# Nyström attention feeding a mixture of experts: the C path's scores for both head halves in one group, the expert chosen on all partitions, and a plan with measured group times

## Chip, cores and metric

One core of a Trainium2 chip runs the whole kernel. The metric is the device time of one execution in microseconds, and for several runs their median. "Rows" below are lines of the profile of one execution. TensorE is PE (its weight loads are PEld), VectorE is DVE, ScalarE is ACT, GpSimd is POOL, SyncE is SP.

## What is computed

The reference takes q, k and v of 4 batches, 8 heads, 576 tokens and 64 columns, and forms landmarks as means over 18 tokens, 32 for each head:

```python
A = sm(q, k_lm)
Bm = sm(q_lm, k_lm)
C = sm(q_lm, k)
Z = Bm.transpose(0, 1, 3, 2) / (norm1 * norminf + 1e-06)
for _ in range(6):
    Z = 2 * Z - Z @ Bm @ Z
x = A @ Z @ C @ v          # (4 * 576, 512)
```

`sm` is a softmax over the last axis of the scaled product, with the row maximum taken off first. The 2304 rows then go through a mixture of 8 experts with a capacity of 576 each: the gate `x @ w_gate` picks one expert a token, tokens past an expert's capacity are dropped, and the output is the token's probability times `relu(x @ w1[e]) @ w2[e]`.

## The kernel before

**Tiling.** Eight heads lie in two halves `x` (or `g`) of 64 partitions, times four places `j` in the free dimension; the product of a 64-row half with 32 landmarks uses a 64x32 tile of TensorE. For each batch `b` six generators issue the work: `loads`, `landmarks`, `chain` (the inverse, six steps `pp`), two `cpath` (C and its product with v), two `apath` (A, by token halves), `route` (gate, expert choice, capacity). For each of the first three batches a feed-forward pass runs with the one expert that most of the batch chooses: `w1load`, `gstage`, `ffn` with its two layers (`hps`, `yps`), `wload`, `wsplit`. The expert is guessed on the chip: `guess` for batch 0 from sums over v, `count` (inside `route`) for batches 1 and 2, both ending in `pick`, which leaves the number `ei` (with it the weights are fetched) and a row `fst` of eight flags on one partition. Batch 3 has no pass of its own here; its output rows are zeroed, and a branch behind the plan would run whatever is left over.

**The C path before.** `cpath(b, g)` runs once for each head half. Eight products of 288 columns (L494) fill a two-bank tile `psC`; VectorE takes the maximum over all 576 tokens (L499) and scales it (L501); ScalarE takes the exponential with its sum (L504); four transposes and a fifth for the last 64 tokens (L524) bring it to tokens on partitions, copied out by L529 and L533; twenty products with v (L541) fill `cvp`, and L546 drains it, times the inverse sum from L509 and L510. The landmark product `mtp` (L605) needs both halves' result and the finished inverse (L480). The A path (L563) takes both halves in one group, for one half of the tokens at a time.

**Expert row.** `fsp` (L699) is a product with ones that copies `fst` to all partitions just before the factors of the output rows (L702) are formed.

**Order.** The order of work is planned before the kernel runs: `weave` (L83) simulates five queues (P for TensorE, V, A, G, and D for transfers) with a cost for every step, hops between engines (`HOP`) and priorities from `CFG`, and emits each instruction when its step is chosen, so each engine's instruction order is what the plan gave it. The strings in `CFG` choose an engine for steps that have a choice (`lm` for the landmark sums, `aw`, `al`, `ce`, `rx`, `lo`, `ye`). `sw` is a penalty on a TensorE step whose kind (FFN or other) differs from the one before. Where the plan sees TensorE idle, `fill` (L923) puts dummy products `wps` (L929) into the gap, one for each 216 ns of it, until the first product of the second FFN layer is issued.

Of the kernel before, what the change touches and what calls it, by code (L numbers as in the profile page):

```python
# [18 lines left out]
class Step:  # L19
    def __init__(self, eng, cost, deps=(), order=(), name=None, res=None, nres=1, keep=False, free=None, prev=True, start=0, prio=None, fast=False,  # L20
                 port=False, issue=430):
        self.issue = issue
# [6 lines left out]
    sw=4000,  # L29
    sc='VAAA',  # L30
    rx='VGVGVVVGGVGVVVVVGGGVVGGGGGGVVGVVGVVGVVVVVGGVGVGV',
    look=0.05,
    tg='fftftfttttfttftfttfttttt',
    ce='AAAVAVAV',
    pa='ffsssfff',
    aw='GVGVGGVGVVGGVVGV',
    ye='VVAAAVVAAAVAAVAV',
    lm='VVVVVGGGGVGVGVVV',
    al='GVGVVG',
    lo='VGVVVGVVGVGVVVGGVVVVVGVV',  # L40
    pr=[
# [4 lines left out]
    ],  # L46
    fr=[
        [-1093, 102, -1718, 504, 1080, 901],
        [-5297, 910, -3998, 1924, 1728, -3915],
        [-5242, -5815, -509, 4290, -4277, 441],  # L50
    ],
    sp=[-640, -5473, -5831],
    ah=[-5437, -2470, -2263],
    rl=[-485, -2407, -4653],
    ev=[596, -2196, 1681],
)
HOP = dict(P=205, V=85, A=105, G=0, D=2000)
# [25 lines left out]
def weave(streams, banks, fill=None):  # L83
# [7 lines left out]
    fast = False  # L91
# [21 lines left out]
    while ready:  # L113
# [21 lines left out]
        t, s = min((c for c in cand[eng] if c[0] <= lim), key=lambda c: (c[1][5] + swap * (c[1][2].fast != fast), c[0]))  # L135
# [4 lines left out]
        if eng == "P":  # L140
            if step.fast != fast:
                t += 60
            fast = step.fast
# [7 lines left out]
        t = end + HOP[eng] if step.cost else end  # L151
# [20 lines left out]
def nystrom_moe(ctx: ExitStack, tc: tile.TileContext, q, k, v, vtail, wgate, w1, w2, out, cap):  # L172
# [59 lines left out]
    wg = const.tile([128, NP, NG, 32], F32, name="wg")  # L232
# [45 lines left out]
    def loads(b):  # L278
# [3 lines left out]
        for g in range(2):  # L282
            for nm, src in (("q", q), ("k", k)):
                busy = ([f"psA{b - 2}0", f"psA{b - 2}1", f"psC{b - 2}0"] if nm == "q" else
                        [f"psC{b - 2}0", f"psC{b - 2}1", f"psA{b - 2}0"])
                for j0, j1 in ((2 * g, 2 * g + 1), (2 * g + 1, 2 * g + 2)) if one else ((2 * g, 2 * g + 2),):
                    yield Step("D", 820 * (j1 - j0), deps=[*busy, f"bp{b - 2}"] if b > 1 else (), prev=False,
# [74 lines left out]
    def guess(b):  # L362
# [3 lines left out]
        for x in range(NG):  # L366
            for ch in range(2):
                if x or ch:
                    yield Step("P", 300, prev=False, deps=[f"ld{b}{x}v"], name=f"gs{b}" if x and ch else None)
# [629 lines left out]
```

## Time and profile before

| | |
|---|---|
| Median of 3 runs | 205.97 us (205.31 to 206.12) |
| The profiled execution | 205.63 us, span 203.9 us |
| TensorE matmul busy | 196.2 us, 96% (of it the dummies of L929: 23.2) |
| VectorE busy | 127.9 us, 63% |
| ScalarE busy | 78.0 us, 38% |
| GpSimd busy | 66.0 us, 32% |
| DMA | 31.95 MB, 157 GB/s mean |

Busy time of TensorE includes the dummies and is modelled at the ends of pipelined matmuls, so it tells less than the other engines' figures; the mean duration of one matmul is longer than the step from one to the next. The chain of waits joins the pieces of work that ended last, so the length of a piece there is the time that it takes out of the span.

### The profile page before, as it was taken

To read this page: it belongs to the slowest core of one execution; us is meant where nothing else is said; L and a number is where in the kernel's file an instruction comes from. 1 tells how busy PE (TensorE), PEld (TensorE's weight loads), DVE (VectorE), ACT (ScalarE), POOL (GpSimd) and SP (SyncE) were. 2 spreads that over 40 slices of the span, in tenths; PEclk is the share of its full clock that TensorE was granted. 3 is DMA by queue.
4 is the path that set the end of the run, shared out by engine and by line. 5 is a ranking of instruction groups with operands and counts; after the bars stand their busy time and mean duration, and the time that the engine had idled before them with its cause. 6 is when DMAs were issued, how large, how long until landed. Compare 5 with 4: busy or idle time off the path is not lost.

```text
span 203.9 us, 5705 instructions
## 1 busy us (share of the span) xinstructions
PE 196.2 (96%) x2301; PEld 140.1 (69%) x2302; DVE 127.9 (63%) x381; ACT 78.0 (38%) x178; POOL 66.0 (32%) x110
## 2 busy tenths in 40 slices
PE   7999999999999999999999999999999999999980
PEld 2435454757787766776887776777887789788870
DVE  3789964899798686947888678794024685200100
ACT  2014142944762213326486555410155757111000
POOL 7017599850610238326167453000000506000000
PEclk9999999999999999999999999999999999999998
DMA  6999799934500159897563095301117000020021
GB/s 204 387 412 359 273 293 393 320 95 148 158 3 0 26 167 318 291 359 239 169 206 120 0 301 217 108 17 63 51 51 257 5 3 2 3 67 31 35 82 37
DMA packets 17924, 31.95 MB, mean 157 GB/s; under 512 B 1568, under 2 KB 9632, under 8 KB 17888
## 3 DMA queue, kind: packets, MB, share of 16 engines
q1 hardware_dynamic: 17744, 31.46, 44.9%
q8 instruction: 20, 0.33, 0.7%
q14 instruction: 16, 0.13, 0.2%
q10 hardware_dynamic: 144, 0.03, 0.1%
HBM read 26.77 MB, written 4.72 MB: 154 GB/s over the span
## 4 chain that ended last, share of the span: by engine, by line
PE 94%; DVE 3%; ACT 0%; issue 0%
PE yps L874 33%; PE hps L816 21%; PE wps L929 10%; PE yps L879 5%; PE psC L494 4%; PE pp L471 3%; PE gps L596 3%; PE cvp L541 3%; PE ctp L524 3%; PE psA L563 3%; PE ltp L641 1%; PE bbp L454 1%; PE mtp L605 1%; DVE lmq L329 1%; PE bp L402 1%; PE pp L468 1%
## 5 line engine op out<-in xcount | busy, mean ns | idle before, releaser
L874 PE MATMUL yps<-wh,hx 128*128 128x512 f32 (+1 forms) x208 | 62.8, 378 | 0.0
L874 PEld LDWEIGHTS yps<-wh,hx 128*128 128x128 f32 x208 | 38.1, 189 | 8.1 <-issue 0.5
L874 PE MATMUL yps<-wl,hx 128*128 128x512 f32 (+1 forms) x104 | 38.8, 373 | 0.0
L816 PE MATMUL hps<-ah,gh 128*128 128x288 f32 x96 | 30.5, 318 | 0.0
L839 POOL TENSOR_TENSOR hx<-rr,hx 128x288 fp32r<-128x288 f32 (+2 forms) x31 | 19.4, 645 | 28.3 <-ACT hx L830 23.2
L816 PE MATMUL hps<-al,gh 128*128 128x288 f32 x96 | 28.3, 295 | 0.0
L816 PE MATMUL hps<-ah,gl 128*128 128x288 f32 x96 | 28.3, 295 | 0.0
L929 PE MATMUL wps<-wt 128*128 128x512 bf16 x87 | 23.2, 404 | 1.3 <-DVE half L222 1.3
L874 PEld LDWEIGHTS yps<-wl,hx 128*128 128x128 f32 x104 | 19.6, 188 | 3.3
L889 ACT ACTIVATE yo<-yps,fac 128x512 f32<-128x512 f32 (+1 forms) x9 | 6.0, 666 | 40.5 <-PE yps L874 37.9
L816 PEld LDWEIGHTS hps<-ah,gh 128*128 128x128 f32 x96 | 18.0, 188 | 3.6 <-ACT hx L830 1.0
L755 POOL TENSOR_TENSOR wl<-w2t,wh 128x512 fp32r<-128x512 f32 x7 | 9.1, 1295 | 33.8 <-ACT wh L749 33.7
L755 DVE TENSOR_TENSOR wl<-w2t,wh 128x512 fp32r<-128x512 f32 x17 | 12.6, 749 | 9.7 <-issue 9.3
L816 PEld LDWEIGHTS hps<-al,gh 128*128 128x128 f32 x96 | 18.1, 188 | 0.0
L816 PEld LDWEIGHTS hps<-ah,gl 128*128 128x128 f32 x96 | 18.0, 188 | 0.0
L929 PEld LDWEIGHTS <-wt 128*128 128x128 bf16 x87 | 8.1, 103 | 11.6 <-issue 4.2
L891 DVE TENSOR_SCALAR yo<-yps,fac 128x512 f32<-128x512 f32 (+1 forms) x4 | 2.7, 684 | 20.1 <-PE yps L874 20.1
L841 DVE SCALAR_TENSOR_TENSOR hx<-hps,hx 128x224 fp32r<-128x224 f32 (+2 forms) x41 | 13.1, 348 | 2.9 <-ACT hx L833 2.6
L749 ACT CAST wh<-w2t 128x512 fp32r<-128x512 f32 x24 | 14.4, 617 | 0.9 <-DMA w2t<-in_w 0.7
L833 ACT ACTIVATE hx<-hps 128x288 fp32r<-128x288 f32 x27 | 11.1, 410 | 9.1 <-PE hps L816 8.8
L504 ACT ACTIVATE Cx<-psC,cs 128x576 f32<-128x576 f32 x8 | 5.9, 743 | 19.6 <-DVE cs L501 19.6
L775 ACT CAST gh<-gps 128x512 fp32r<-128x512 f32 x12 | 7.0, 587 | 13.3 <-PE gps L596 13.2
(173 smaller groups left out, 323.1 us busy)
## 6 DMA issues: line engine op xcount, KB each, us to landing
w1t<-in_w SPq DMA_DIRECT2D x12, 512.0 KB, 5.5
w2t<-in_w SPq DMA_DIRECT2D x24, 256.0 KB, 5.8
vm<-in_v SPq DMA_DIRECT2D x8, 512.0 KB, 7.0
qt<-in_q SPq DMA_DIRECT2D x6, 576.0 KB, 6.8
kt<-in_k SPq DMA_DIRECT2D x6, 576.0 KB, 7.6
out<-yo SPq DMA_DIRECT2D x11, 256.0 KB, 2.0
qt<-in_q SPq DMA_DIRECT2D x4, 288.0 KB, 4.6
kt<-in_k SPq DMA_DIRECT2D x4, 288.0 KB, 5.7
```

The lines of the kernel that those rows point to most:

```text
L471: nc.tensor.matmul(pp[y, x], lhsT=PQ[y, x, 0], rhs=PQ[y, x, 0:3:2], start=True, stop=True)
L494: nc.tensor.matmul(t[32 * j:32 * j + 32, a, :HS], lhsT=lmt[b]["q"][y, j], rhs=st[b]["k"][y, j, HS * a:HS * a + HS], start=True, stop=True)
L749: nc.scalar.copy(wh, w2t)
L755: (nc.gpsimd if e == "G" else nc.vector).tensor_tensor(wl, w2t, wh.bitcast(F32), ALU.subtract)
L775: nc.scalar.copy(gh, pg[:, :, 0:FH])
L816: nc.tensor.matmul(ps[:, :HS], lhsT=wt[:, g, fs], rhs=a[:, g, ss], start=(n == 0), stop=(n == 3 * NG - 1))
L833: nc.scalar.activation(hx[:, fc, ss], ps[:, :HS], AF.Relu)
L839: nc.gpsimd.tensor_tensor(dst, rr[:, x0 - s0:x1 - s0], hi, ALU.subtract)
L841: nc.vector.scalar_tensor_tensor(dst, ps[:, x0 - s0:x1 - s0], 0.0, hi, ALU.max, ALU.subtract)
L874: nc.tensor.matmul(ps[:, :dn], lhsT=hx[:, fc, o:o + 128], rhs=wt[:, d0:d1], start=(fc == 0 and o == t0 and wt is wh), stop=(fc == NFC - 1 ...
L879: nc.tensor.matmul(ps[:m], lhsT=hx[:, fc, t0:t0 + m], rhs=wt, start=(fc == 0 and wt is wh), stop=(fc == NFC - 1 and wt is wh))
L929: nc.tensor.matmul(wps[0], lhsT=wt[:, 0:128], rhs=wt, start=True, stop=True)
```

## The change

- **C path.** `cpath(b, a)` now takes a piece of tokens (0 to 255, then 256 to 575) for both head halves in one group, as the A path does, eight products into two banks. Each piece has its own maximum for each half and its own exponentials, one for each half. Transposes are two groups of four and one of two. `cjoin` joins the two maxima, turns each piece's maximum into a factor with one small exponential, and forms the joint sum. `cval` runs the value products with a separate accumulation for each piece, and drains them with two operations in place of one.
- **Choice of expert.** The products of `guess` and `count` broadcast their one-column operand to 128 columns, so `pick` runs on all partitions; `fst` is there on all of them, and `fsp` goes. The gate product has a third group of 32 columns (all heads together), from which `count` needs one product in place of two.
- **Plan.** TensorE steps have kinds (S, R for FFN, T, B) with costs that are measured group times, a hop by kind (`PHOP`), a charge for each turn from one kind to another (`TURN`), and a rebate for a group of the same form (`SAME`). `sw` falls from 4000 to 500 and counts kinds; `look` goes to 0; all engine strings and priorities are new. The costs of many steps rise, the score groups of C from 260 + 260 to 560 and 670.
- **Loads.** Both value loads of a batch wait for the last drain of the batch before.

The core of the diff; the old `cpath` is in the code printed above, and the new strings and priorities that are left out follow the same pattern.

```diff
--- before.py
+++ after.py
-    sw=4000,
-    sc='VAAA',
...
-    look=0.05,
...
-    lm='VVVVVGGGGVGVGVVV',
...
+    sw=500,
+    sc='VVAA',
+    rx='VGGVGVVVVGVVVVGVGGVVVVVGVVVGVGGVVVGVGVVGGVGVGVVV',
+    look=0,
...
+    lm='VVGVVVGVVGGVGGGV',
...
-HOP = dict(P=205, V=85, A=105, G=0, D=2000)
+HOP = dict(V=85, A=105, G=0, D=2000)
+PHOP = dict(S=70, R=165, T=245, B=150)
+TURN = dict(RS=90, RT=105, TS=174, BS=100, TT=60)
+SAME = dict(a=137, c=100)
...
-        t, s = min((c for c in cand[eng] if c[0] <= lim), key=lambda c: (c[1][5] + swap * (c[1][2].fast != fast), c[0]))
+        t, s = min((c for c in cand[eng] if c[0] <= lim),
+                   key=lambda c: (c[1][5] + swap * (last is not None and c[1][2].kind != last.kind), c[0]))
...
-            if step.fast != fast:
-                t += 60
-            fast = step.fast
+            if last is not None:
+                turn = TURN.get(last.kind + step.kind, 0) - (SAME[last.tag] if last.tag and last.tag == step.tag else 0)
+                t = max(s[4] if turn < 0 and t <= clk["P"] else t, clk["P"] + turn)
+            last = step
...
-        t = end + HOP[eng] if step.cost else end
+        t = end + (PHOP[step.kind] if eng == "P" else HOP[eng]) if step.cost else end
...
-    wg = const.tile([128, NP, NG, 32], F32, name="wg")
+    wg = const.tile([128, NP, NG + 1, 32], F32, name="wg")
...
-    onef = const.tile([128, 128], F32, name="onef")
+    onef = const.tile([128, 1], F32, name="onef")
...
-    fst = [keep.tile([1, E], F32, name=f"fst{b}") for b in range(B - 1)]
+    fst = [keep.tile([128, E], F32, name=f"fst{b}") for b in range(B - 1)]
...
+    cse = [keep.tile([128, NG, 3], F32, name=f"ce{i}") for i in range(2)]
+    for t in cse:
+        nc.vector.memset(t[:, :, 2:3], 1e-9)
...
-            yield Step("D", 1640, deps=[f"cv{b - 1}{x}", *(["gs0"] if b == 1 else [])] if b else (), name=f"ld{b}{x}v", prev=False)
+            yield Step("D", 1640, deps=[f"cv{b - 1}", *(["gs0"] if b == 1 else [])] if b else (), name=f"ld{b}{x}v", prev=False)
...
-        gm = sm.tile([1, 1], F32, tag="gm", name="gm")
+        gm = sm.tile([128, 1], F32, tag="gm", name="gm")
...
-        nc.vector.tensor_scalar(fst[b], rev[0:1], fx, None, op0=ALU.is_equal)
+        nc.vector.tensor_scalar(fst[b], rev, fx, None, op0=ALU.is_equal)
...
-        p = Step("P", 200, res="tp", keep=True, deps=["wg"])
+        p = Step("P", 913, kind="T", res="tp", keep=True, deps=["wg"])
         yield p
-        gl = ptp.tile([1, E], F32, tag="tp", name="glg")
+        gl = ptp.tile([128, E], F32, tag="tp", name="glg")
         for i in range(4):
-            nc.tensor.matmul(gl, lhsT=vsb[:, i:i + 1], rhs=wgs[:, i // 2, i % 2], start=(i == 0), stop=(i == 3))
+            nc.tensor.matmul(gl, lhsT=vsb[:, i:i + 1].to_broadcast([128, 128]), rhs=wgs[:, i // 2, i % 2], start=(i == 0), stop=(i == 3))
...
-            p = Step("P", 220, res="ch", keep=True)
+            p = Step("P", 417 if last else 356, res="ch", keep=True)
...
+    csx, csf = {}, {}
+
+    def cpath(b, a):
+        s0, s1 = (0, 256) if a == 0 else (256, S)
+        n = s1 - s0
+        nj = 2
+        p = Step("P", 560 if a == 0 else 670, tag="a", res="sc", keep=True,
+                 deps=LM(b, "q") + [f"ld{b}k{j}" for j in range(4)], name=f"psC{b}{a}",
+                 order=[f"ct{b - 1}{a}", f"cv{b - 1}"] if b else ())
         yield p
         t = psc.tile([128, 2, 512], F32, tag="sc", name="psC")
+        for j in range(4):
+            for x in range(NG):
+                y = slice(64 * x, 64 * x + 64)
+                nc.tensor.matmul(t[32 * j:32 * j + 32, x, :n], lhsT=lmt[b]["q"][y, j],
+                                 rhs=st[b]["k"][y, j, s0:s1], start=True, stop=True)
+        yield V(60 + 2 * n)
+        if b not in csx:
+            csx[b] = (sm.tile([128, 2, NG, 2], F32, tag="cs", name="cs"), cse[b % 2])
+        cs, sums = csx[b]
+        nc.vector.tensor_reduce(out=cs[:, 0, :, a], in_=t[:, :, :n], axis=AX.X, op=ALU.max)
         yield V(65)
+        nc.vector.tensor_scalar(cs[:, 1, :, a], cs[:, 0, :, a], -SC1, None, op0=ALU.mult)
+        Cx = at.tile([128, NG, n], F32, tag=f"C{a}", name="Cx")
+        for x in range(NG):
+            yield Step("A", 250 + n * 5 // 6, free=p if x else None, start=0 if x else 60,
+                       name=[f"cx{b}{a}"] * x)
+            nc.scalar.activation(Cx[:, x, :], t[:, x, :n], AF.Exp, bias=cs[:, 1, x, a:a + 1], scale=SC1,
+                                 accum_out=sums[:, x, a:a + 1])
+        CT = at.tile([128, NG, nj + a, 128], F32, tag=f"CT{a}", name="CT")
+        st[b][f"CT{a}"] = CT
+        tag, pool = small(6 * b + a)
+        p = Step("P", 412, kind="T", res=tag, keep=True)
+        yield p
+        pt = pool.tile([128, NG, nj, 128], F32, tag=tag, name="ctp")
+        for x in range(NG):
+            for i in range(nj):
+                nc.tensor.transpose(pt[:, x, i, :], Cx[:, x, 128 * i:128 * i + 128], ident)
+        e = CFG["ce"][2 * b + a]
+
+        def evac(pt=pt, e=e):
+            (nc.scalar.copy if e == "A" else nc.vector.tensor_copy)(CT[:, :, 0:nj, :], pt)
+
+        later(evac, e, 478 if e == "A" else 600, free=p, name=f"ct{b}{a}")
+        if a:
+            tag, pool = small(6 * b + 2)
+            p = Step("P", 110, kind="T", res=tag, keep=True)
             yield p
+            pt = pool.tile([128, NG, 128], F32, tag=tag, name="ctq")
+            for x in range(NG):
+                nc.tensor.transpose(pt[:lastv * (x + 1), x, :], Cx[:, x, n - lastv * (x + 1):n], ident)
+            for x in range(NG):
+                r = slice(lastv * x, lastv * x + lastv)
+                yield Step("A", 160, free=p if x else None, name=[f"cu{b}"] * x)
+                nc.scalar.copy(CT[r, x, nj, :], pt[r, x, :])
+
+    def cjoin(b):
+        yield V(70, deps=[f"cx{b}0", f"cx{b}1"], prev=False, port=True)
+        cs, sums = csx.pop(b)
+        cm = sm.tile([128, 2, NG], F32, tag="cm", name="cm")
+        cf = csf[b] = sm.tile([128, 2, NG, 2], F32, tag="cf", name="cf")
+        nc.vector.tensor_tensor(cm[:, 0], cs[:, 0, :, 0], cs[:, 0, :, 1], ALU.max)
+        yield V(70, port=True)
+        nc.vector.tensor_tensor(cf[:, 0], cs[:, 0], cm[:, 0].unsqueeze(2).to_broadcast([128, NG, 2]), ALU.subtract)
+        yield Step("A", 150)
+        nc.scalar.activation(cf[:, 0], cf[:, 0], AF.Exp, scale=SC1)
+        yield V(70, port=True)
+        nc.vector.tensor_tensor(sums[:, :, 0:2], sums[:, :, 0:2], cf[:, 0], ALU.mult)
+        yield V(70)
+        nc.vector.tensor_reduce(out=cm[:, 1], in_=sums, axis=AX.X, op=ALU.add)
+        yield V(80)
+        nc.vector.reciprocal(cm[:, 1], cm[:, 1])
+        yield V(70, port=True, name=f"cg{b}")
+        nc.vector.scalar_tensor_tensor(cf[:, 1], cf[:, 0], -1.0, cm[:, 1].unsqueeze(2).to_broadcast([128, NG, 2]),
+                                       ALU.mult, ALU.mult)
+
+    def cval(b):
+        for x in range(NG):
+            tag, pool = small(6 * b + 3 + x)
+            p = Step("P", 830, res=tag, deps=[f"ld{b}{x}v", f"ld{b}vl", f"ct{b}0", f"ct{b}1", f"cu{b}"], keep=True, prev=False)
+            yield p
+            cvp = pool.tile([128, 2, 64], F32, tag=tag, name="cvp")
+            for j in range(5):
+                c, i = (0, j) if j < 2 else (1, j - 2)
+                k = slice(lastv * x, lastv * x + lastv) if j == 4 else slice(0, 128)
+                for h in range(4):
+                    nc.tensor.matmul(cvp[32 * h:32 * h + 32, c, :], lhsT=st[b][f"CT{c}"][k, x, i, 32 * h:32 * h + 32],
+                                     rhs=st[b]["v"][x][j][:, h, :], start=(i == 0), stop=(j == 1 or j == 4))
+
+            def cvf(x=x, p=p, cvp=cvp):
+                yield V(130, deps=[f"cg{b}"], order=[f"mt{b - 2}"] if b > 1 else ())
+                CV = sm.tile([128, D], F32, tag=f"CV{x}", name="CV")
+                st[b][f"CV{x}"] = CV
+                cf = csf[b]
+                nc.vector.tensor_scalar(CV, cvp[:, 0, :], cf[:, 1, x, 0:1], None, op0=ALU.mult)
+                yield V(130, free=p, name=[f"cv{b}{x}"] + [f"cv{b}"] * x)
+                nc.vector.scalar_tensor_tensor(CV, cvp[:, 1, :], cf[:, 1, x, 1:2], CV, ALU.mult, ALU.add)
+
+            spawned.append(cvf())
...
-        p = Step("P", 209, res="ch", keep=True, deps=[f"wd{b}"] + [f"cv{b}{g}" for g in range(NG)])
+        p = Step("P", 369, res="ch", keep=True, deps=[f"wd{b}"] + [f"cv{b}{g}" for g in range(NG)])
...
+            nc.gpsimd.tensor_copy(wg[:, :, NG, 0:E], wga[:, 1])
...
-                p = Step("P", 100, res="tp", keep=True)
+                p = Step("P", 240, kind="T", res="tp", keep=True)
                 yield p
-                gl = ptp.tile([1, E], F32, tag="tp", name="glg")
-                for g in range(NG):
-                    nc.tensor.matmul(gl, lhsT=onef[:, 0:1], rhs=Gg[:, g, 0:E], start=(g == 0), stop=(g == NG - 1))
+                gl = ptp.tile([128, E], F32, tag="tp", name="glg")
+                nc.tensor.matmul(gl, lhsT=onef.to_broadcast([128, 128]), rhs=Gg[:, NG, 0:E], start=True, stop=True)
...
-            p = Step("P", 60, res="ch", keep=True, deps=[f"fs{b}"])
-            yield p
-            fsp = pch.tile([128, E], F32, tag="ch", name="fsp")
-            nc.tensor.matmul(fsp, lhsT=onef[0:1], rhs=fst[b], start=True, stop=True)
-            yield V(125, free=p)
+            yield V(125, port=True, deps=[f"fs{b}"])
             f1 = sm.tile(sh, F32, tag="f1", name="f1")
-            nc.vector.tensor_tensor(f1, f, fsp.unsqueeze(1).to_broadcast(sh), ALU.mult)
+            nc.vector.tensor_tensor(f1, f, fst[b].unsqueeze(1).to_broadcast(sh), ALU.mult)
...
-        parts = [loads(b), landmarks(b), chain(b), route(b), cpath(b, 0), cpath(b, 1), apath(b, 0), apath(b, 1)]
+        parts = [loads(b), landmarks(b), chain(b), route(b), cpath(b, 0), cpath(b, 1), apath(b, 0), apath(b, 1), cjoin(b), cval(b)]
```

## Rows read from the trace of the kernel before

**Rows 1.** The page: TensorE's busy tenths in forty slices of the span

```profile
PE   7999999999999999999999999999999999999980
```

**Rows 2.** Busy time by stage: length, PE, PEld, DVE, ACT, POOL, clock, DMA share, GB/s

```profile
9.60:37.20 27.60, 27.16 (x459) 13.05 (x459) 22.01 (x68) 8.54 (x19) 17.87 (x24) 1.00 0.93 343
...
43.90:141.50 97.60, 97.60 (x1348) 71.69 (x1345) 77.86 (x227) 44.20 (x102) 32.98 (x38) 1.00 0.47 153
```

**Rows 3.** The same of line 929 on TensorE alone: length, PE, clock, DMA, GB/s

```profile
9.60:37.20 27.60, 12.99 (x50) 1.00 0.93 343
37.20:43.90 6.70, 1.90 (x8) 1.00 0.74 246
43.90:203.90 160.00, 0.00 (x0) 1.00 0.34 113
```

**Rows 4.** Chain of waits, early stage: start, length (us), engine, tile, line, count

```profile
24.92 0.36 PE pp L471 x16
...
30.91 0.89 PE psC L494 x12
...
32.12 0.37 PE mtp L605 x4
32.49 0.75 PE wps L929 x3
33.24 0.25 PE gp L622 x8
```

**Rows 5.** VectorE in order of time: start, length, line, operation, count

```profile
20.26 0.14 DVE L350 TENSOR_REDUCE gm<-glg 1x1 f32<-1x8 f32 x1
...
24.24 0.29 DVE L476 TENSOR_TENSOR PQ<-pp,PQ 128x128 f32<-128x128 f32 x1
...
30.98 0.28 DVE L546 TENSOR_SCALAR CV<-cvp,cs 128x64 f32<-128x64 f32 x1
...
32.56 0.29 DVE L608 COPY MT<-mtp 128x128 f32<-128x128 f32 x1
```

**Rows 6.** Chain of waits, the small groups of TensorE in the late stage

```profile
53.89 1.10 PE psC L494 x16
...
57.58 0.65 PE psA L563 x16
58.23 0.59 PE ctp L524 x4
...
63.04 0.31 PE fsp L699 x2
63.36 0.26 PE ctp L524
...
81.07 0.17 PE glg L632 x4
```

**Rows 7.** TensorE in order of time, the guess for batch 0

```profile
17.48 0.35 PE L382 MATMUL glg<-wga,vsb 128*1 128x8 f32 x8
```

**Rows 8.** Chain of waits, stretches of FFN matmuls, the first and the last among them

```profile
37.19 3.36 PE hps L816 x24
...
48.45 1.00 PE hps L816 x6
...
165.61 6.57 PE hps L816 x48
...
175.86 22.10 PE yps L874 x120
```

**Rows 9.** Groups by line: count, busy us, mean ns of one, idle before

```profile
L499 DVE TENSOR_REDUCE cs<-psC 128x1 f32<-128x576 f32 x8 | 6.0, 748 | 1.9 <-PE psC L494 1.6
...
L504 ACT ACTIVATE Cx<-psC,cs 128x576 f32<-128x576 f32 x8 | 5.9, 743 | 19.6 <-DVE cs L501 19.6
...
L546 DVE TENSOR_SCALAR CV<-cvp,cs 128x64 f32<-128x64 f32 x8 | 2.2, 273 | 0.0
L504 ACT ACTIVATION_READ_ACCUMULATOR Cx<-psC,cs 128x1 f32 x8 | 1.6, 194 | 0.0
```

More of the change, by code (lines that the diff above doesn't have):

```diff
@@ L90, in weave @@
     wait = {}
-    fast = False
+    last = None
     def enable(s):
@@ L395, in chain @@
         PA = PQs[b % 2]
-        p = Step("P", 170, deps=LM(b), order=[f"wd{b - 2}", f"mt{b - 2}"] if b > 1 else (), name=f"bp{b}", res="sc", keep=True)
+        p = Step("P", 222, deps=LM(b), order=[f"wd{b - 2}", f"mt{b - 2}"] if b > 1 else (), name=f"bp{b}", res="sc", keep=True)
         yield p
@@ L481, in chain @@
         st[b]["Wd"] = Wd
-    def cpath(b, g):
-        p = Step("P", 260, res="sc", keep=True,
-                 deps=LM(b, "q") + [f"ld{b}k{j}" for j in range(4)],
-                 order=[f"cv{b - 1}{i}" for i in range(NG)] if b else ())
+    csx, csf = {}, {}
[6 more added lines that the diff above has]
+                 order=[f"ct{b - 1}{a}", f"cv{b - 1}"] if b else ())
@@ L487, in cpath @@
         yield p
         t = psc.tile([128, 2, 512], F32, tag="sc", name="psC")
-        y = slice(64 * g, 64 * g + 64)
-        for a in range(2):
-            if a:
-                yield Step("P", 260, name=f"psC{b}{g}", prev=False)
-            for j in range(4):
-                nc.tensor.matmul(t[32 * j:32 * j + 32, a, :HS], lhsT=lmt[b]["q"][y, j],
-                                 rhs=st[b]["k"][y, j, HS * a:HS * a + HS], start=True, stop=True)
-        yield V(660)
-        ps = t[:, :, :HS]
@@ L506, in cpath @@
-        CT = at.tile([128, 5, 128], F32, tag="CT", name="CT", bufs=2)
-        def rsum():
-            nc.vector.tensor_scalar(cs[:, 3:4], cs[:, 2:3], 1e-9, None, op0=ALU.add)
-            nc.vector.reciprocal(cs[:, 3:4], cs[:, 3:4])
-        later(rsum, "V", 260, name=f"cr{b}{g}")
-        for j0, n in ((0, 4), (4, 1)):
-            tag, pool = small(6 * b + 3 * g + j0 // 4)
-            p = Step("P", 500 if n == 4 else 128, res=tag, keep=True)
-            yield p
-            pt = pool.tile([128, 4, 128], F32, tag=tag, name="ctp")
-            r = slice(0, 128) if j0 == 0 else slice(lastv * g, lastv * g + lastv)
-            for i in range(n):
-                s0 = 128 * (j0 + i)
-                s1 = s0 + 128
-                if j0:
-                    s0, s1 = S - lastv * (g + 1), S
-                nc.tensor.transpose(pt[:s1 - s0, i, :], Cx[:, s0:s1], ident)
-            if j0 == 0:
-                e = CFG["ce"][2 * b + g]
-                def evac(pt=pt, e=e):
-                    (nc.scalar.copy if e == "A" else nc.vector.tensor_copy)(CT[:, 0:4, :], pt)
-                later(evac, e, 478 if e == "A" else 600, free=p, name=f"ct{b}{g}")
@@ L532, in cpath @@
-        yield Step("A", 160, free=p)
-        nc.scalar.copy(CT[r, 4, :], pt[r, 0, :])
-        tag, pool = small(6 * b + 3 * g + 2)
-        p = Step("P", 520, res=tag, deps=[f"ld{b}{g}v", f"ld{b}vl", f"ct{b}{g}"], keep=True)
-        yield p
-        cvp = pool.tile([128, 64], F32, tag=tag, name="cvp")
-        for j in range(5):
-            k = r if j == 4 else slice(0, 128)
-            for h in range(4):
-                nc.tensor.matmul(cvp[32 * h:32 * h + 32, :], lhsT=CT[k, j, 32 * h:32 * h + 32],
-                                 rhs=st[b]["v"][g][j][:, h, :], start=(j == 0), stop=(j == 4))
@@ L552, in apath @@
         two = CFG["pa"][2 * b + a] == "f"
-        p = Step("P", 250, res="f" if two else "sc", nres=2 if two else 1, deps=deps, order=order, name=f"psA{b}{a}", keep=True)
+        p = Step("P", 646, tag="a", res="f" if two else "sc", nres=2 if two else 1, deps=deps, order=order, name=f"psA{b}{a}", keep=True)
         yield p
@@ L950, in nystrom_moe @@
             with tc.If(again > 0):
-                for part in (loads(b), landmarks(b), chain(b), cpath(b, 0), cpath(b, 1), apath(b, 0), apath(b, 1),
-                             mpart(b)):
+                for part in (loads(b), landmarks(b), chain(b), cpath(b, 0), cpath(b, 1), cjoin(b), cval(b), apath(b, 0),
+                             apath(b, 1), mpart(b)):
                     run(part)
```

85 lines of the change are left out of this document (36 added, 49 removed), and 8 rows, old and new, of the table pr.

## Prediction

> **What bounds the kernel now.** I read the page's forty slices first: from the second slice to the end of TensorE's work the busy digit is 9 [rows 1], at a granted clock of 1.00 [rows 2]. A row of nines says little as long as dummy matmuls count as work, so the second view was the busy time by stage, and the third the same stages for line 929 alone, which issues the dummies. The kernel falls apart in two. Between 9.6 and 37.2 us, where batch 0's attention runs and the first expert is fetched, TensorE is busy 27.16 of 27.60 us, but 12.99 of that is dummies, while VectorE works 22.01 us and the DMA engines 0.93 of the time [rows 2, 3]. That stage is bound by a chain of small steps that hops between engines, at a VectorE nearly full. In the next 6.7 us there are 1.90 us of dummies, and from 43.9 us on none at all [rows 3]: there TensorE runs real work back to back, and any real matmul time removed there comes off the end. So I price the change in two sums: matmul time after 43.9 us, and how early that stage can begin.
>
> **The profiled run against the others.** The sums go against the profiled execution, 205.63 us with a span of 203.9. The median of the runs shown is 205.97, so I add 0.34 at the end.
>
> **Late sum, scores of the C path.** Before, one group handles one head half and takes 1.10 us for two pieces of 288 columns, two groups to a batch, 2.20 us. The A path does the same products with both halves in one group: 0.65 us for 288 columns of both [rows 6]. The change gives C that form in pieces of 256 and 320 tokens. Scaling by columns, 0.65 x 256/288 = 0.58 and 0.65 x 320/288 = 0.72, together 1.30, so 0.45 less for each group. Of the six groups of batches 1 to 3 one runs before 43.9 us (at 30.91) [rows 4]; the other five give 5 x 0.45 = 2.25 us. Bounds: nothing, if the halves do not overlap, and half the time, 5 x 0.55 = 2.75. I take the A row, which is the same operation on the same shapes but for the column count.
>
> The Trainium skill, TensorEngine Tiling (Array Packing), section Theoretical Speedup, gives up to 2x when the contraction is 64 rows or less. By it the two pieces would take 1.10 us a batch, the far bound just named. The row with its 0.65 us shows a little less than that.
>
> **Late sum, the other matmul groups.** The broadcast of the chosen expert over partitions goes: 0.31 us [rows 6], three times, since the row is now built on all partitions: 0.93 less. Transposes: a batch had two groups of four (0.59) and two of one (0.26); now two of four and one of two. Taking half of 0.59 for two, 0.52 - 0.30 = 0.22 less a batch, and for two and a half batches 0.55; the bounds are 0 and 2 x 0.26 x 2.5 = 1.3. Added: the count that chooses the expert, 0.17 us [rows 6], twice, now with 128 weight columns. The removed broadcast also loads 128 columns in two halves and takes 0.31, so 2 x 0.14 = 0.28 more; no gain is likely, since weight columns only rise. The gate product widens from 64 to 96 columns, 0.25 us now [rows 4]; at most half more, I take 0.06 each, three times 0.2. The value products keep their 40 entries. Late sum: 2.25 + 0.93 + 0.55 - 0.28 - 0.2 = **3.25 us less**, with bounds of 0.9 - 0.9 = 0 and 4.5.
>
> **Early sum.** The planner puts dummies where it thinks TensorE idles, and it thinks so with costs that are too low: it counts 220 for a step of the inverse that takes 0.36 us and 260 + 260 for the 1.10 us score group, so real time runs behind its clock and dummies overrun. The chain of waits against VectorE's own order shows it: the first step of the inverse has its operand at 24.24 + 0.29 = 24.53 and starts at 24.92; the landmark product has its last operand at 30.98 + 0.28 = 31.26 and starts at 32.12; the gate product has it at 32.85 and starts at 33.24, after 0.75 us of dummies [rows 4, 5]. Seven such steps lie between the first and the last of these, and their lateness beyond a hop sums to about 2.7 us (an estimate, the first 0.34 and the landmark product 0.81 among them). With measured costs (356 for 220, 560 and 670 for the scores) the dummies fit better. I take half, **1.4 us less**. The floor is nothing; the ceiling is 2.7 plus the 1.90 us of dummies after 37.2, or 4.6. A loss is possible too, below.
>
> **What lies beside other work.** The first expert's guess loads four weights of 128 columns instead of one column. I bound it from 0 to 2 us more: 0.35 us for eight entries now, and the 0.31 us of the two-entry broadcast four times. It lies behind cover: it ends at 17.83, and its reader, the maximum on VectorE, starts only at 20.26 [rows 5, 7]. Without that cover the weight loads would wait by as much. VectorE: the maxima keep their elements (0.75 us for 576), the sum of the exponentials needs no separate steps, but the join adds six small operations and the value step doubles to four of 0.27. Net four more small ones a batch, 0.14 to 0.27 each [rows 5, 9], 2 to 4 us in all beside an engine that works 77.86 of the 97.60 us after 43.9 [rows 2]: no cost there. ScalarE goes from two exponentials to four, each between half of 0.74 and 0.74, and two more accumulator reads of 0.19: 0.4 to 1.9 us a batch, on an engine with the larger part of its time free. In the early stage those VectorE operations do count; against them the new assignment gives one of batch 0's four landmark sums and one A-path multiplication to GpSimd, about 0.75 x 2 each way, so I take zero, and -1.5 to +2 for the range.
>
> **New waits.** Both value products now wait for both pieces and the last transposes; their drain waits for the join (two VectorE operations, a small exponential, four more). Behind that drain, on VectorE, stands whatever the planner has put next. Both value loads of the next batch wait on SP's queue for the last drain, where one half used to go earlier; weight loads stand behind them on that queue. Early this meets DMA engines at 0.93 busy [rows 2], so a later issue mostly queues less; after 43.9 the fetches run ahead. I price both at 0 and leave up to 1 us.
>
> **Rivals.** (1) *More alternation, slower than before.* Six matmuls of the first FFN layer take 1.00 us when they stand alone between small groups, and 6.57/8 = 0.82 each in a run of 48 [rows 8]: each interruption costs about 0.18. After 37 us the chain has 31 unbroken stretches of FFN matmuls (the first and the last piece stand in the rows), against some 75 small groups that could each interrupt. The change lowers the planner's penalty for alternating from 4000 to 500, with priorities spread over +-10000. Twenty more interruptions cost 3.6 us and eat the late sum; if the early stage gains nothing, the kernel is slower by over 0.5% from 3.25 + 1.03 = 4.3 us on, 24 more. All 44 more would give 205.97 - 3.25 + 7.9 = 210.6. For it: the penalty. Against: the new planner charges 90 to 174 for such turns, and there are fewer small groups.
>
> The Trainium skill, TensorEngine Tiling (Array Packing), section Key Properties, says that a change of tiling mode drains TensorE. The rows' 0.18 us agree with that, and no run here separates the drain from the rest.
>
> (2) *The chain only moves.* The join and four exponentials lengthen batch 0's path on a VectorE 80% busy, and the early gain is nil: 205.97 - 3.25 = 202.7. The same if halves overlap less: without overlap, 205.0. For it: VectorE's 22.01 of 27.60. Against: the join runs beside transposes and value products. (3) *The order gives all*: 205.97 - 3.25 - 4.6 = 198.1. (4) *The scores do not overlap* although the code asks for it: 2.25 of the late sum goes, 203.6 with the early gain. The A row speaks against it.
>
> **How the numbers follow.** 205.63 - 3.25 - 1.4 = 200.98, plus 0.34 for the median: 201.3. Measurement tells 0.5% (1.0 us) from no change. Forecast (199.5 to 202.3): 0.42. Order gives all, 197.5 to 199.5: 0.12. Chain only moves or scores do not overlap, 202.3 to 204.9: 0.19. Alternation eats most, 204.9 to 207: 0.13; more than all, over 207: 0.14. So faster 0.73, same 0.13, slower 0.14. The range takes in all but the slowest case and half of the one before: 197.5 to 206.0.
>
> **What would show it.** Score groups on TensorE near 0.58 and 0.72 us; no broadcast group; transposes of the tail once a batch; under 13 us of dummies in all after 9.6 us, and the dummies ending before 43.9; the first FFN matmul before 37.2; 31 FFN stretches or fewer. Wrong would be: idle slices on TensorE after 44 us, 60 stretches, or a first FFN matmul at 39 us or later.

## The result, and the profile after

The changed kernel takes 199.53 us (median of 4, 199.37 to 200.41) against 205.98 us (median of 4, 205.31 to 206.12): a ratio of 0.970, interval 0.967 to 0.974. That is 6.45 us less where 4.7 was forecast (201.3), inside the range. Its profiled execution took 199.64 us with a span of 197.9; the last matmul starts at 191.75 us, where it started at 197.67 before.

The page of the changed kernel, TensorE's busy tenths (to be held against [rows 1]):

```profile
PE   7989979999999999999999999999999999999980
```

The nines now have holes in the first quarter: TensorE stands still there, where before dummies kept it busy (1.08 us of it is a stop for which the profile names no wait, see the last section). The stages of the changed kernel, in the columns of [rows 2]:

```profile
9.60:37.20 27.60, 24.71 (x463) 13.71 (x474) 24.44 (x69) 9.46 (x25) 12.57 (x16) 1.00 0.98 364
...
43.90:141.50 97.60, 96.71 (x1381) 71.01 (x1381) 79.03 (x263) 43.85 (x110) 36.71 (x48) 1.00 0.45 149
```

The dummies alone (line 968 now), in the columns of [rows 3]:

```profile
9.60:37.20 27.60, 9.16 (x35) 1.00 0.98 364
37.20:43.90 6.70, 0.00 (x0) 1.00 0.78 240
```

12.99 us of dummies became 9.16 and 1.90 became none; VectorE's busy time in the early stage rose from 22.01 to 24.44 us. The chain of waits of the changed kernel in the early stage, to be held against [rows 4]:

```profile
30.87 0.37 PE mtp L648 x4
31.24 0.54 PE wps L968 x2
31.78 0.59 PE gps L639 x16
32.37 0.30 PE gp L666 x8
...
34.51 2.58 PE hps L855 x18
```

The landmark product comes at 30.87 in place of 32.12 and the FFN's first layer begins at 34.44 (the matmul's own start) in place of 36.94. The weights are asked for sooner too: the expert is chosen at 19.24 + 0.13 us, and the first weight transfer is issued at 21.85, where the kernel before issued it at 24.45. Below, VectorE and SyncE in order of time in the changed kernel, and after them SyncE of the kernel before:

```profile
19.24 0.13 DVE L366 TENSOR_SCALAR ei<-fx 1x1 int32<-1x1 f32 x1
...
21.85 1.58 SPq L769 DMA_DIRECT2D w1t<-in_w  x3
```

```profile
24.45 1.65 SPq L730 DMA_DIRECT2D w1t<-in_w  x3
```

The prediction measured the dummies' overrun as the time by which a group starts after its operand is ready. The same reading of the changed kernel, VectorE in order of time first and the chain of waits after it:

```profile
20.54 0.29 DVE L484 TENSOR_TENSOR PQ<-pp,PQ 128x128 f32<-128x128 f32 x1
...
29.31 0.47 DVE L587 SCALAR_TENSOR_TENSOR CV<-cvp,cf,CV 128x64 f32<-128x64 f32 x2
```

```profile
21.02 0.35 PE pp L479 x16
...
29.20 1.67 PE wps L968 x7
```

At the second step of the inverse the lateness fell from 24.92 - 24.53 = 0.39 to 21.02 - 20.83 = 0.19 us; over all six steps, by their starts in TensorE's own order, it fell from 1.8 to 0.6 us. At the landmark product it rose: the operand is there at 29.31 + 0.47 = 29.78 us and the product comes at 30.87, behind seven dummies, 1.09 us late where it was 0.86 late before. So the dummies fit better in the inverse and still overrun ahead of the landmark product.

The small groups of the late stage, in the chain of waits, answer to [rows 6]:

```profile
67.44 0.70 PE psC L505 x16
...
71.47 0.30 PE gp L666 x8
71.80 0.67 PE psC L505 x16
72.47 0.59 PE ctp L528 x4
73.05 0.12 PE glg L675 x2
...
73.53 0.34 PE ctq L541 x2
```

Now the whole difference. For each matmul I took the time from its start to the start of the next, and summed that by tile, in both profiled executions. The last matmul's end moved by 5.92 us, of which

| part | us |
|---|---|
| first FFN matmul, 36.94 to 34.44 | -2.50 |
| dummies after it | -1.83 |
| scores of C, 5 groups in 5.52 to 6 groups in 3.86 | -1.66 |
| broadcast of the flags | -0.94 |
| w1 products (one group moved ahead of the FFN's start) | -0.70 |
| transposes, 3.39 to 2.88 + 0.47 | -0.04 |
| gate product and expert count | +0.36 |
| FFN matmuls, waits among them | +0.84 |
| other small groups, waits among them | +0.57 |

(w1 products: the products `gps` of the first weights with the landmark result.) TensorE's idle time after the first FFN matmul rose from 0.00 to 1.14 us; that accounts for most of the last two lines. The two largest single waits stand in the changed kernel's TensorE and VectorE in order of time:

```profile
104.18 0.66 PE L577 MATMUL cvp<-vm,CT 128*32 128x64 f32 x32 [0.41 <-DVE sel L361]
...
110.33 0.42 PE L479 MATMUL pp<-PQ 32*32 32x64 f32 x16 [0.37 <-DVE fac L723]
```

```profile
102.64 1.15 DVE L746 TENSOR_SCALAR rest<-rest 1x8 f32<-1x8 f32 x1
103.71 0.15 DVE L358 TENSOR_REDUCE gm<-glg 128x1 f32<-128x8 f32 x1
...
103.89 0.23 DVE L361 SCALAR_TENSOR_TENSOR sel<-glg,gm,rev 128x8 f32<-128x8 f32 x1
```

The value product needs the PSUM bank that the expert choice frees at L361, and that stands on VectorE behind an operation on eight numbers that took 1.15 us (more on it at the end). That operation stood in the kernel before too; it is none of those that the change adds.

### The profile page after: what moved, and what is told of

Read it like the earlier page. It is cut to its first block, busy times and chain, and to the rows that moved or that the text cites. A ratio compares the mean times of both kernels' runs of the same rounds, so it can differ in the third digit from the quotient of the medians.

```text
span 197.9 us, 5686 instructions
## 1 busy us (share of the span) xinstructions
PE 186.7 (94%) x2267; PEld 136.4 (69%) x2273; DVE 127.7 (65%) x406; ACT 78.3 (40%) x191; POOL 65.5 (33%) x110
## 4 chain that ended last, share of the span: by engine, by line
PE 86%; DVE 9%; issue 2%; ACT 0%; DVEq 0%
PE yps L913 33%; PE hps L855 19%; PE wps L968 8%; PE yps L918 6%; PE gps L639 4%; PE pp L479 4%; PE cvp L577 3%; PE psC L505 2%; PE psA L606 2%; PE ctp L528 2%; PE ltp L684 1%; DVE amx L618 1%; DVE wl L794 1%; DVE AW L613 1%; PE mtp L648 1%
## 5 line engine op out<-in xcount | busy, mean ns | idle before, releaser
L913 PE MATMUL yps<-wh,hx 128*128 128x512 f32 (+1 forms) x208 | 63.5, 379 | 0.0
L878 POOL TENSOR_TENSOR hx<-rr,hx 128x288 fp32r<-128x288 f32 (+2 forms) x24 | 15.2, 650 | 30.8 <-ACT hx L869 30.8
L880 DVE SCALAR_TENSOR_TENSOR hx<-hps,hx 128x224 fp32r<-128x224 f32 (+2 forms) x48 | 14.9, 343 | 7.1 <-ACT hx L872 6.8
L968 PE MATMUL wps<-wt 128*128 128x512 bf16 x63 | 17.5, 418 | 1.9 <-DVE half L227 1.3
L794 POOL TENSOR_TENSOR wl<-w2t,wh 128x512 fp32r<-128x512 f32 x6 | 7.8, 1309 | 32.7 <-ACT wh L788 32.7
L872 ACT ACTIVATE hx<-hps 128x288 fp32r<-128x288 f32 x31 | 12.7, 410 | 7.0 <-PE hps L855 6.8
L794 DVE TENSOR_TENSOR wl<-w2t,wh 128x512 fp32r<-128x512 f32 x18 | 13.3, 759 | 1.5 <-ACT wh L788 1.4
L968 PEld LDWEIGHTS <-wt 128*128 128x128 bf16 x68 | 6.3, 104 | 9.6 <-issue 3.9
L631 POOL TENSOR_TENSOR AW<-AW,amx 128x576 f32<-128x576 f32 x5 | 6.1, 1219 | 14.8 <-DVE cf L564 7.9
L518 ACT ACTIVATE Cx<-psC,cs 128x256 f32<-128x256 f32 (+1 forms) x16 | 7.9, 498 | 5.2 <-DVE cs L513 3.6
```

Of the source, the lines that this page charges most:

```text
L518: nc.scalar.activation(Cx[:, x, :], t[:, x, :n], AF.Exp, bias=cs[:, 1, x, a:a + 1], scale=SC1, accum_out=sums[:, x, a:a + 1])
L794: (nc.gpsimd if e == "G" else nc.vector).tensor_tensor(wl, w2t, wh.bitcast(F32), ALU.subtract)
L872: nc.scalar.activation(hx[:, fc, ss], ps[:, :HS], AF.Relu)
L878: nc.gpsimd.tensor_tensor(dst, rr[:, x0 - s0:x1 - s0], hi, ALU.subtract)
L880: nc.vector.scalar_tensor_tensor(dst, ps[:, x0 - s0:x1 - s0], 0.0, hi, ALU.max, ALU.subtract)
L913: nc.tensor.matmul(ps[:, :dn], lhsT=hx[:, fc, o:o + 128], rhs=wt[:, d0:d1], start=(fc == 0 and o == t0 and wt is wh), stop=(fc == NFC - 1 ...
```

## Experiments

The theory: the gain is matmul time that leaves the late stage, plus a chain that reaches the FFN sooner because dummies no longer hold it back. The rivals: the scores were covered and only the order counts; the early chain waits for VectorE whatever the dummies do; the join takes back what the scores give. In the experiments on scores, dummies, join and broadcast below the order of instructions on all engines is kept, but for the instructions that the edit names; in the other four the planner orders the work anew. Times are held against the 199.53 us above. The kernel before, timed beside these runs, took 205.54 to 205.77 us where it took 205.98 beside the changed kernel, so a difference of a few tenths says nothing. Nor does one of half a microsecond in the start of the FFN in a single execution: the run with three products added, which changes nothing ahead of that start, has it at 33.97 in place of 34.44.

**Scores issued twice (203.4 to 204.7 expected by the theory).**

```diff
-        for j in range(4):
+        for j in [0, 1, 2, 3, 0, 1, 2, 3]:
             for x in range(NG):
```

> The changed kernel in its own order, with each of the eight score groups of the C path issued twice (the second copy writes the same values, so only time is added). Theory, real matmul work in the late stage comes off the end one for one: six groups run after the first FFN matmul, in their trace 3.86 us together, so 199.5 + 3.9 = 203.4 us; batch 0's two groups, 1.3 us, stand in the early chain and may add up to as much, 204.7. Rival, the gain comes from the order and the scores are covered by waits: under 200.5 us.

Measured 204.15 us (203.18 to 204.99), 4.6 more than the changed kernel. The first FFN matmul starts at 34.52, as before the edit, but batch 0's two extra copies are not shown to be covered: the value products ahead of it start 1.29 us later, and what makes up for that is that the stop of 1.08 us inside them is absent in this execution. The chain of waits, the changed kernel and then this run:

```profile
25.94 1.14 PE cvp L577 x46
```

```profile
27.23 1.73 PE cvp L577 x80
```

In the late stage its chain shows two of the six groups:

```profile
47.92 1.24 PE psC L505 x32
...
74.02 1.02 PE psC L505 x32
```

Scores in the late stage went from 3.86 to 6.95 us. The profiled execution (204.99 us, the slowest of the four) lost some 2 us more: TensorE idles 2.76 us after the FFN's start, against 1.14, and 1.25 of that is one stop at 89.67 us with no wait named. By the median, 4.6 us in all, what the late scores do not explain is about 1.5.

**The two halves kept from running side by side** (the first half's scores are formed twice, the second half's are left out).

```diff
-                y = slice(64 * x, 64 * x + 64)
+                y = slice(0, 64)
```

> The changed kernel in its own order, every instruction in its place, but both halves' scores read the rows of the first head half, so that the two halves' products use the same rows of the array and cannot run side by side (the second half's scores are left out, the first half's computed twice). Theory, the gain of the joint group is this overlap: each late group back by 0.46 us, six of them 2.8 us, 199.5 + 2.8 = 202.3; with batch 0's two in the early chain up to 203.2. Rival, the gain is the order's: 199.5 to 200.

Measured 203.66 us (203.65 to 204.23), 4.1 more. The chain of waits:

```profile
69.89 1.23 PE psC L505 x16
74.74 1.02 PE psC L505 x16
```

The same sixteen entries take 1.23 in place of 0.70 and 1.02 in place of 0.67, together 2.25, as much as the two groups of a batch took before the change (2.20). So the gain of the joint group is the overlap of the halves on different rows of the array. The late groups' sum grows by 2.88 (3.86 to 6.74), the first FFN matmul comes 0.76 later, and most of the rest is waits (1.80 us idle in place of 1.14). The time is above the 203.2 that was the theory's upper end, and the rival "covered by waits" falls.

**The kernel before with half the dummies.**

```diff
         if st[0].get("y"):
             return
+        n = n if not wps else n // 2
```

> The kernel before in its own order, with every gap's count of dummies after the first lot halved (57 become 25). Theory, dummies overran and held back the early chain: the first FFN matmul comes 1.4 us earlier (between 0.7 and 3), and the dummies between 37 and 44 us give up to 0.9 more: 205.98 - 1.4 = 204.6 us. Rival, the chain waits for VectorE and the transfers and the dummies only fill: 205.5 to 206.1 us.

Measured 203.92 us (203.65 to 205.12), 1.65 below the 205.57 of the kernel before in the same runs. TensorE in order of time:

```profile
35.05 0.38 PE L816 MATMUL hps<-ah,gh 128*128 128x288 f32 x1
```

36.94 became 35.05: dummies alone held the early chain back by 1.9 us, with nothing else changed. The first weight transfer is issued at 23.62 us in place of 24.45.

**The changed kernel with more, none, and half of its dummies.** The same place as above, with `2 * n + 1` (where n is not 0), `0` and `n // 2`.

> The changed kernel in its own order, with every gap that gets n dummies after the first lot getting 2n + 1. Theory, overrunning dummies hold the chain back: each of the roughly ten gaps grows by its own length and one more, the first FFN matmul comes 2 to 5 us later and the end with it, 201.5 to 204.5 us. Rival, TensorE has slack in the early stage (2.9 us idle in the 27.6 after 9.6 us): within 0.7 us of 199.5.

> The changed kernel in its own order, with no dummies after the first lot. Theory, after the change the dummies fit their gaps: the time stays within 1 us of 199.5 as long as the granted clock holds, and the first FFN matmul comes at most 1 us earlier. Rival, they still overrun: 2 us or more faster. Third case, the granted clock falls to its lower level in the early stage and the small groups there lengthen: 200.5 to 203 us.

> The changed kernel in its own order, every gap's dummies after the first lot halved (some 30 become under 15). Theory, a few dummies still overrun (seven of them, 1.67 us, end just as the landmark product begins): first FFN matmul 0.3 to 0.9 us earlier, 198.9 us. Rival, they fit: 199.5. Third case, the granted clock falls as it did with no dummies: 201 to 204.

*More*: 206.23 us (204.56 to 207.31), 6.7 more. Dummies of line 969 in the stage of [rows 3], and the start of the FFN in the chain of waits:

```profile
9.60:37.20 27.60, 17.44 (x75) 1.00 0.89 331
```

```profile
41.66 2.58 PE hps L855 x18
```

Nearly twice the dummies' time cost the FFN 7.15 us, and the late stage then runs in the same 157.3 us (157.6 before the edit): what the start loses here, the end loses. The theory's upper bound of 204.5 was too low: some 10.6 us of dummies were added ahead of the FFN (8.28 of them in this stage), and the chain lost 7.15 of that.

*None*: 204.30 us (203.64 to 205.46). The third case, though above the 203 that it was given: the granted clock falls. Busy time by stage, in the columns of [rows 2]:

```profile
9.60:20.00 10.40, 9.16 (x124) 5.45 (x122) 8.52 (x31) 1.93 (x7) 5.21 (x7) 0.83 0.95 379
20.00:30.00 10.00, 8.76 (x203) 5.53 (x206) 8.21 (x24) 3.68 (x10) 0.16 (x1) 0.50 0.76 270
30.00:37.20 7.20, 5.23 (x83) 2.63 (x80) 6.40 (x14) 1.95 (x4) 5.50 (x7) 0.74 1.06 383
37.20:43.90 6.70, 6.45 (x75) 5.37 (x75) 4.22 (x14) 4.49 (x12) 4.79 (x6) 0.76 0.89 288
```

Between 20 and 30 us TensorE runs at 0.50, its lower level of 1.2 GHz, the inverse's steps stretch, and the FFN starts at 36.33, 1.9 us later. The low clock also reaches into the FFN. The first eighteen of its matmuls in this run's chain of waits, which take 2.58 us in the changed kernel:

```profile
36.40 4.42 PE hps L855 x18
```

That is 1.8 us more. In the profiled execution (205.46 us) the last matmul ends 5.5 us later than in the changed kernel; the rest of that, 1.8 us, was lost after these matmuls.

*Half*: 200.69 us (200.15 to 202.74), 1.2 more, a miss for both theories, which foresaw no loss. The FFN starts 1.5 us earlier, at 32.92, more than the 0.3 to 0.9 expected, and still ends 1.0 us later. The late stage loses 2.6 us: 1.25 in a stop that the profile puts down to nothing, and 0.7 behind a VectorE operation that took 1.41 us where the same line takes 0.21 in the changed kernel. TensorE and VectorE in order of time, and then TensorE's waits (us in total, times, longest):

```profile
86.00 0.47 PE L684 MATMUL ltp<-AT,Gg 128*32 128x160 f32 x4 [1.25 <-issue]
```

```profile
38.43 1.41 DVE L429 TENSOR_TENSOR BB<-BB,bst 128x64 f32<-128x64 f32 x1
```

```profile
PE bbp L462 <- DVE BB L435: 0.7, 1, 0.7
```

So none of the three other numbers was faster than the change's own. That half is worse in itself isn't shown, since its 1.2 us are less than the stop of 1.25 without a cause: fewer dummies do bring the FFN forward.

**The join left out.** `cjoin` issues only `nc.vector.memset(cf[:, 1], 1.0)` at its first step.

> The changed kernel in its own order with the join of the maxima left out (no joint maximum, factors or sum; the value drain multiplies by one constant). Six small VectorE operations and one exponential a batch go, a single fill of the factors stays. Theory, the join lies beside transposes and value products: 199.5 - 0.5, between 198.5 and 199.7. Rival, it lengthens the chain that feeds the landmark product in the early stage: 197.5 or less.

Without the factors the leftover branch behind the plan runs, so the whole time (459 us) says nothing; the planned part can still be read from the trace. The FFN starts at 34.57 (34.44 with the join), and the last matmul of the plan stands here in TensorE's order of time, against 191.75 with the join:

```profile
192.15 0.28 PE L906 MATMUL yps<-wh,hx 128*128 128x256 f32 x1
```

The join costs nothing that one execution can show: no earlier start, no earlier end, and TensorE idles 0.97 us between the FFN's start and the plan's end, against 1.14. The join's part of rival 2 is nil.

**Three products of the removed broadcast's form.**

```diff
+        if b < B - 1:
+            nc.tensor.matmul(rp[:, 0, :], lhsT=onef[0:1].to_broadcast([1, 128]), rhs=rev[0:1], start=True, stop=True)
         nc.tensor.matmul(rp, lhsT=ones, rhs=carry[:, b, :].unsqueeze(1)
```

> The changed kernel in its own order with one product of the removed broadcast's form (one row of ones, 128 weight columns, 8 columns moved) put in front of the capacity count of batches 0 to 2, its result unread. All three stand after the first FFN matmul. Theory: 3 x 0.31 = 0.9 us more, 200.4. Rival, covered by waits on VectorE: 199.5.

Measured 201.18 us (200.16 to 202.78), between 0.6 and 3.2 more in the single executions. Each stands in the chain of waits:

```profile
50.46 0.31 PE rp L712 x2
...
97.15 0.31 PE rp L712 x2
...
107.52 0.31 PE rp L712 x2
```

In the profiled execution (200.16, whose FFN happens to start 0.47 us earlier) the late stage grew by 0.70 us, 0.93 of products less some wait. What the slower two executions lost beyond it was not profiled.

**Plan and code taken apart.** Four kernels in which the planner ran anew: the kernel before with the new rules and costs only; the kernel before with the whole new plan; the changed code under the old plan; and the changed kernel with the flag broadcast back as a planned step.

```diff
 # changed code, flag broadcast back
+            p = Step("P", 220, kind="T", res="ch", keep=True, deps=[f"fs{b}"])
+            yield p
+            fsp = pch.tile([128, E], F32, tag="ch", name="fsp")
+            nc.tensor.matmul(fsp, lhsT=onef[0:1].to_broadcast([1, 128]), rhs=fst[b][0:1], start=True, stop=True)
```

> The kernel before with nothing of the C path or the expert choice changed, but with the planner's new rules and measured costs (kinds, turns, hops); engine strings, priorities and the penalty of 4000 stay. Theory, better fitting dummies are the early gain: 205.98 - 1.4 = 204.6, between 203 and 206. Rival, costs alone reorder the work at random around strings and priorities that were fitted to other costs: 206 to 210.

> The kernel before with the whole new plan: rules, measured costs, strings and the priorities of the eight generators that both kernels have, penalty 500. Theory, plan and code add up: the plan alone gives the early gain and no late one, about 203 us. Rival, the order was fitted to the new code and does not carry over: slower than 206.

> The changed C path and expert choice under the old planner: old rules, old costs, old strings and priorities, penalty 4000 (the two new generators at the smaller of the two C path priorities). Theory, the late sum comes from the code alone: 205.98 - 3.25 = 202.7 us, between 201.5 and 204.5. Rival, without a fitted order nothing is left of it: 205.5 or more.

> The changed kernel with the product that broadcasts the flag row put back (three groups of 0.31 us, read from PSUM as before). Theory, each stands in the late stage: 199.5 + 0.94 = 200.5 us if the order stays, with up to 1 us either way because the planner sees the added step. Rival, hidden: 199.5.

Measured 226.27, 208.05, 244.20 and 204.75 us. None of the four theories held. The rivals held for the second and the third; the first lies far above even its rival's 206 to 210, and the fourth above both of its cases (200.5 with up to 1 us either way, and 199.5). The stage from 43.9 to 141.5 us of the first (costs only) and the third (old plan), in the columns of [rows 2]:

```profile
43.90:141.50 97.60, 85.47 (x1173) 61.89 (x1174) 64.57 (x187) 38.53 (x88) 29.19 (x35) 0.90 0.45 154
```

```profile
43.90:141.50 97.60, 81.67 (x1083) 55.98 (x1082) 62.56 (x194) 34.43 (x85) 20.15 (x25) 0.88 0.38 128
```

Here TensorE does wait, 12 and 16 us of the 97.6, and its clock is no longer granted in full. Even three planned steps of 0.22 us each turn the order over: with the broadcast back the FFN starts at 34.02, but its matmuls are cut into 37 stretches in place of 31, TensorE idles 3.54 us after the start in place of 1.14, and 5.2 us are lost, of which the three products account for 0.9 to 1.4. In these four kernels an order fitted to one set of steps did not carry to another, so they give no separate shares of code and plan in the 6.45 us that could be added.

## Why the prediction was right

**The split** into a late sum and an early start was right: with more dummies the late stage kept its length while the start moved by 7 us. The fit is not exact: with half the dummies the start came 1.5 us earlier and the late stage grew by 2.6.

**Early sum: mis-sized.** I took 1.4 us of lateness and nothing of the 1.90 us of dummies after 37.2, with a ceiling of 4.6. It came to 2.50 + 1.83 = 4.3, close to the ceiling. The mechanism is shown on the kernel before: half the dummies, 1.9 us earlier. It is not the whole of the 2.50. In the changed kernel the overrun went out of the inverse (1.8 to 0.6 us) but grew at the landmark product (0.86 to 1.09), and 1.08 us of the early chain is a stop without a cause that the kernel before did not have. What I had left out is that the early chain as a whole begins sooner: the expert is chosen 4.1 us earlier, its weights are asked for 2.6 us earlier (0.8 of it comes with half the dummies alone), and the inverse starts 3.7 us earlier. That the earlier fetch brought the FFN forward isn't shown: in the changed kernel the weight loads of the first product with these weights wait for the landmark result, and no transfer is among TensorE's waits. Its weight loads' waits:

```profile
PEld gps L639 <- DVE MT L651: 0.4, 1, 0.4
```

How much of the earlier start is due to better costs and how much to new engine strings stays open, since the run with costs alone lost its order.

**Late sum: right by group, too high in the net.** A score group gave 0.46 us (0.45 taken), and the two experiments on scores put it on the path; but six groups run late where I had counted five, so the scores gave 1.66 in place of 2.25. The broadcast gave 0.94 (0.93 taken). The transposes saved 0.13 a batch over the whole run (5.29 to 4.76 us) against 0.22 taken, but only 0.04 us after the FFN's start, because groups of batch 1 that ran before it now run after it, as the sixth score group does. A group of w1 products (0.70 us) moved the other way, and I had none of these moves in the sum. The term that was mis-sized most is the late stage's waits, taken as nothing: TensorE now stands idle 1.14 us where it had 0.00, and the two largest waits end with VectorE. That the four more VectorE operations a batch cause them isn't shown. Without the join, which is six of the added operations, 0.97 us of idle time remain and the end comes no earlier; and the wait at 104 us stands behind an operation that the kernel before had too. What the new order puts behind what on VectorE is the likelier cause, and no run separates it.

Net the late sum gave 1.6 us where 3.25 was expected. The two errors, 2.9 us too little early and 1.7 us too much late, have opposite signs, and that they offset each other in part is luck. Of the 1.8 us by which the total came out beyond the forecast they leave 1.3; the rest is mostly the 0.34 us added for the median, which after the change lies 0.11 below the profiled execution.

**The other steps.** Expert count and gate product cost 0.36 (0.48 taken). The guess's weight loads lengthened the group (from 0.28 to 0.88 us) and stayed hidden, as said: it ends at 17.8 us and its reader starts at 18.35. The join was free, as far as one execution shows. That both value loads now wait for the last drain was not tested by itself; no transfer is among TensorE's waits in the changed kernel. The Trainium skill, TensorEngine Tiling (Array Packing), section Theoretical Speedup, allows up to 2x for halves side by side; the groups measured 1.23 against 0.70 and 1.02 against 0.67 us, 1.5 to 1.8 times.

**Rivals.** Alternation did not come: 31 stretches before and after, though the penalty fell to 500. It was no idle fear, as the kernel with the broadcast back has 37. The scores' overlap is real. For the early stage "the order gives all" was the nearest of the cases, at 4.3 of 4.6.

## What to carry to other kernels

Where one engine does real work back to back, time that a group leaves on it comes off the end, and can be summed from the trace by group, less the waits that a new order brings. Where filler keeps the engine busy, sum the filler's overrun first, by the time that the operand was ready against the time that the group began. Here every order that was fitted to one set of steps lost when a step came or went, so "one part undone" is a test only if the order is held fixed. That measured group times make a better plan isn't shown: the run with these alone lost 20 us.

## What the runs showed of the hardware

**A small VectorE operation can wait out a GpSimd operation.** The 1.15 us of L746 on eight numbers (the line's other two instances in the changed kernel took 0.16 us) and the 1.41 us of L429 with half the dummies (0.21 in the changed kernel) both end within 0.1 us of the end of a GpSimd operation. GpSimd in order of time, of the changed kernel and of the one with half its dummies:

```profile
102.45 1.32 POOL L794 TENSOR_TENSOR wl<-w2t,wh 128x512 fp32r<-128x512 f32 x1 [3.76 <-ACT wh L788]
```

```profile
38.44 1.32 POOL L343 TENSOR_TENSOR tr<-kt 128x576 f32<-128x576 f32 x1
```

102.45 + 1.32 = 103.77 and 102.64 + 1.15 = 103.79; 38.44 + 1.32 = 39.76 and 38.43 + 1.41 = 39.84. The Trainium skill, SBUF — State Buffer, section Who interferes with whom, says that GpSimd and some VectorE operations share a pair of ports that one of them holds for its whole instruction while the other blocks. The two pairs of rows agree with that; no run here took the GpSimd operation away. The wait of 0.41 us at 104 us stands behind the first of them. In the run without the join the same GpSimd line meets another VectorE operation, and the wait at 104 us is gone.

**TensorE stood still inside a group, with no wait named.** In the changed kernel it happens for 1.08 us within the value products at 27 us, on the early chain, and in four of the runs that keep its order it happens in the same group, for 0.70 to 1.00 us: with half the dummies, with the halves' scores on the same rows, with the three products and without the join. TensorE in order of time, in the changed kernel and with half the dummies:

```profile
26.77 0.31 PE L577 MATMUL cvp<-vm,CT 128*32 128x64 f32 x6
28.16 0.64 PE L577 MATMUL cvp<-vm,CT 128*32 128x64 f32 x26 [1.08 <-issue]
```

```profile
26.62 0.43 PE L577 MATMUL cvp<-vm,CT 128*32 128x64 f32 x16
27.75 0.43 PE L577 MATMUL cvp<-vm,CT 128*32 128x64 f32 x16 [0.70 <-issue]
```

Counted in the traces, 344 matmuls stand ahead of the stop in all five. With half the dummies ten fewer stand ahead of the value products, and the stop falls ten matmuls further into them. So it goes with the place in TensorE's stream of instructions and not with the work done there.

With scores doubled, with more dummies and with none it is absent there, and stops of 1.25 us stand elsewhere with scores doubled (at 89.67 us) and with half the dummies (at 86.00). What is behind it stays open.
